# The row of maxima sent from ScalarE's queue, and a new order of instructions up to tile 2

## The chip, the core and the metric

The kernel runs on one core of a Trainium2 chip. The metric is the device time of one execution in microseconds (us), without the host. A core has TensorE (PE; matrix products, in the profile also PEld, the weight loads), VectorE (DVE), ScalarE (ACT), GpSimd (POOL) and SyncE (SP), which here only issues DMAs. An engine works through its instructions in program order; engines wait for each other through semaphores. DMAs can be issued by SP, ACT and POOL, each on its own queue, and all of them run on the core's 16 DMA engines. Matmul results go to PSUM, eight banks; other tiles lie in SBUF.

## What is computed

Attention with a decay bias over 8 batches, 8 heads, 576 positions and 64 dimensions, then Fourier mixing over positions and channels, a layer norm and an MLP of 512 to 2048 to 512, all in float32:

```python
scores = scale * np.matmul(q, k.transpose(0, 1, 3, 2))
cum = np.cumsum(np.maximum(s, 0.0), axis=-1)
bias = -(cum[:, :, :, None] - cum[:, :, None, :])
scores = np.where(causal, -1000000000.0, scores + np.minimum(bias, 0.0))
scores = scores - np.max(scores, axis=-1, keepdims=True)
attn = np.exp(scores)
attn = attn / (np.sum(attn, axis=-1, keepdims=True) + 1e-09)
x = np.matmul(attn, v)            # heads side by side: 8 x 576 x 512
mixed = np.real(np.fft.fft(np.fft.fft(x, axis=1), axis=2))
u = x + mixed
un = (u - mu) / np.sqrt(var + 1e-06)
out = u + np.maximum(un @ w_ch1, 0.0) @ w_ch2
```

## The kernel before

The 64 heads are worked through as 32 pairs. Of each pair the kernel loads q and k transposed (`qk`, line 947) and rounds them to the high part that TensorE's one-pass float32 takes (`KQ`, `high()`, lines 964 and 966); the rest goes to `q` and `k` (`low()`, lines 981 to 989, partly by DMA), the values to `va` (line 992). `KQ` has 128 partitions: 64 carry the head's dimensions, of the others three carry the bias (`cumD`, line 961) and the maximum, so that one matmul gives q times k plus bias minus maximum.

The maximum has to be known ahead of the scores. `maxes(i)` multiplies q and k once with 128 queries on the partitions (`pm`, line 1005), takes the largest of each row on VectorE (`Mx`, `M`, lines 1007 and 1009), turns the nine columns of maxima into rows on TensorE (`pmt`, line 1038), copies them out of PSUM on ScalarE (`mt`, 9 x 128, line 1040) and writes them by DMA into partition 2 of `KQ` (line 1041). This happens for pairs 1 to 31, 31 sends of 4.5 KB; pair 0 goes another way (line 1031). `scores(i)` computes keys by queries (`ps`, lines 1061, 1062 and 1071), ScalarE takes the exponential (`P`, lines 1063 and 1073), GpSimd cuts the causal corner (line 920). `av(i)` multiplies by the values (`pavA`, `pavB`, lines 1094 and 1097), ScalarE copies the result (`stage`, `sumrow`, lines 1099 to 1102), and SP sends the sums on (line 1105); `recip` and `finish` divide (`rd`, `rb`, `xa`, `xs`, `xr`, lines 1111 to 1139). The pairs overlap: beside the scores of pair i run the maxima of pair i + 1, the rounding of pair i + 2, the values of pair i - 1 and the division of pair i - 2.

In the same stage the weights of the MLP are rounded (`raw`, `we`, `wm`, `wD`, lines 505 to 525), GpSimd loads the tables of the Fourier step (lines 733 to 737), and every fourth pair ends a batch, which is folded and mixed (`folds`, `fourier`, lines 753 to 849). Then come the layer norm (`ln_tile`, lines 579 to 626) and the MLP in nine tiles of 512 tokens (`mlp_tile`; `h` line 660, `zh` and `zl` lines 664 and 665, `acc` lines 673 to 675, `out` line 708). Tiles 0 and 1 are done in two halves of the weights each, tile 2 is the fifth part.

The order of instructions up to the end of tile 2 isn't the order of the code. `order()` takes all instructions traced so far, gives each a duration (`cost()`), plays the five engines through, picks for each engine the next instruction and chains each engine's list, so that the program keeps it. Of those that can start within `SLACK[engine]` ns of the earliest, it takes the one of lowest rank: its place in the code, shifted by `SHIFT[engine, tile]` (seven numbers, one for each phase: the first three pairs, the four turns of pairs to a batch, the last pair, and what follows) and by a draw from `SEED`. `SLOTS` says which buffer or PSUM bank each tile takes. Data dependencies and buffers hold in any order; the tables decide only what goes first. For a DMA the play counts 650 ns on the engine that issues it, 1945 ns until it moves, its transfer on a `link`, and 284 ns until it has landed. Before the change all queues share one `link`. From tile 3 on the instructions follow the code.

The three lines that end `maxes()`:

```python
mt = att.tile([9, 128], F32R, tag="mt", name="mt", bufs=2)
nc.scalar.copy(mt, p[0:9, 0:128])
nc.sync.dma_start(out=flat(qy)[2:3].bitcast(F32).rearrange("o (c t) -> o c t", t=128), in_=mt.bitcast(F32))
```

Of the kernel before, what the change touches and what calls it, by code (L numbers as in the profile page):

```python
# [59 lines left out]
SLACK = {PE: 14.0, ACT: 41.0, POOL: 155.0, SP: 10.0}  # L60
SHIFT = {
    (PE, "acc"): (0, 0, 0, 0, 0, 0, 48), (PE, "h"): (0, 0, 0, 0, 0, 0, -9), (PE, "mu"): (0, 12, 0, 0, 0, 0, 18), (PE, "p"): (0, 0, 0, 0, 2059, 0, 6),
    (PE, "pavA"): (0, 1, -4, 48, 0, 0, 0), (PE, "pavB"): (0, -1, -6, 0, 0, -51, 0), (PE, "pm"): (-1333, -6145, 0, -32, 0, 0, 0),
    (PE, "pmt"): (3, -2, 0, -18, -56, 0, 0), (PE, "ps"): (3, 0, 0, 0, 0, 0, 0), (PE, "pyc"): (0, 0, 0, 0, 0, 5, 5),
    (PE, "pys"): (0, 0, 0, 0, 0, -737, -5), (PE, "pzc"): (0, 0, -4179, 16, 0, -5, 112), (PE, "pzs"): (0, 0, 0, 0, 0, 466, 18),
    (PE, "var"): (0, 0, 0, 0, 0, 541, 70),
    (DVE, "Aw"): (116, 0, 0, 0, 366, -15, 0), (DVE, "De"): (0, 0, 0, 0, 0, -16, 0), (DVE, "Df"): (0, 0, 0, 0, 139, -685, 0),
    (DVE, "Dg"): (0, -773, 0, 0, -190, -12, 0), (DVE, "Do"): (0, -210, 0, 0, 0, 227, 0), (DVE, "Ds"): (0, 6, 0, 0, 729, 17, 0),
    (DVE, "KQ"): (231, 0, 0, 0, 0, 0, 0), (DVE, "M"): (-276, 0, -281, 307, 70, 0, 0), (DVE, "Mx"): (0, -3905, 922, -46, 0, 0, 0),
    (DVE, "cumhl"): (-135, 0, 0, 0, 0, 0, 0), (DVE, "cw"): (352, 0, 0, 0, 0, 0, 0), (DVE, "e"): (0, 0, 0, 0, 446, -421, 0),  # L70
    (DVE, "el"): (0, 0, 0, 0, 0, 492, 0), (DVE, "eps"): (-535, 0, 0, 0, 0, 0, 0), (DVE, "k"): (198, 52, 430, 177, 135, 0, 0),
    (DVE, "m"): (0, 0, 0, 0, 0, 0, 403), (DVE, "ones"): (267, 0, 0, 0, 0, 0, 0), (DVE, "r"): (0, 0, 0, 0, 0, 6609, 0),
    (DVE, "rows"): (0, 0, 0, 0, 487, 0, -94), (DVE, "s"): (0, 0, 0, 0, 0, 0, 5), (DVE, "skip"): (-4, 0, 0, 0, 0, 0, 0),
    (DVE, "sums"): (0, 0, 697, 301, -764, -14, 0), (DVE, "t"): (0, -1413, 0, 0, 0, -122, 2531), (DVE, "tl"): (0, 0, 0, 0, 0, -473, 385),
    (DVE, "trash"): (0, 0, 238, -17, -3399, 0, 0), (DVE, "tt"): (0, 0, 0, 0, 0, 0, 772), (DVE, "u"): (0, -132, 0, 0, 0, 0, 1031),
    (DVE, "ucl"): (0, 3907, 0, 0, 0, 0, 866), (DVE, "wbias"): (263, 0, 0, 0, 0, 0, 0), (DVE, "we"): (22, 37, 88, -98, 29, 0, -193),
    (DVE, "wl"): (0, 0, 0, 0, 0, -12, -374), (DVE, "wm"): (29, -94, 1640, 3733, -32, 0, 1395), (DVE, "xr"): (0, 0, 0, 0, 0, 241, 0),
    (DVE, "ym"): (0, 0, 0, 0, 1034, -117, 1601), (DVE, "yp"): (0, 0, 0, 0, -1302, 0, -140), (DVE, "z"): (0, 0, -37, -850, 0, -61, 69),
    (DVE, "zc"): (0, 0, -295, 30, 0, -124, -270), (DVE, "zl"): (0, 0, 0, 0, 0, 0, 136), (DVE, "zs"): (0, 0, 10, 0, 0, -2535, -181),
    (ACT, "De"): (0, 0, 0, 0, -178, -334, 0), (ACT, "Do"): (0, -181, 0, 0, 0, 21, 0), (ACT, "KQ"): (464, 2119, -62, 56, 0, 0, 0),  # L80
    (ACT, "P"): (1000, 5, 22, -43, 1058, 0, 0), (ACT, "Px"): (-244, -2956, 222, -126, -23, 0, 0), (ACT, "e"): (0, 0, 0, 0, 2330, 69, 0),
    (ACT, "el"): (0, 0, 0, 0, -91, -325, 0), (ACT, "k"): (-171, 0, 0, 0, 0, 0, 0), (ACT, "m"): (0, 0, 0, 0, 0, 0, 353),
# [1 line left out]
    (ACT, "q"): (-336, 0, 0, 0, 0, 0, 0), (ACT, "r"): (0, 0, 0, 0, 0, 309, -145), (ACT, "stage"): (284, 0, 5478, -80, -1805, -180, 0),
    (ACT, "sumrow"): (2, -5148, -306, -9, -13, -511, 0), (ACT, "th"): (0, -86, 0, 0, 0, -306, 553), (ACT, "u"): (0, 909, 0, 0, 0, 0, 683),
    (ACT, "uch"): (0, 157, 0, 0, 0, 0, -1053), (ACT, "we"): (368, 0, -932, 603, 27, 0, 0), (ACT, "wh"): (0, 0, 0, 0, 0, 55, 580),
    (ACT, "yc"): (0, 0, 0, 9, -179, -417, 120), (ACT, "zc"): (0, 0, 4, 50, 0, -548, 0), (ACT, "zh"): (0, 0, 0, 0, 0, 0, 106),
    (ACT, "zs"): (0, 0, 0, 0, 0, 0, 84),
    (POOL, "Bw"): (0, -1371, 0, 0, 6, 0, 0), (POOL, "Dg"): (0, -333, 0, 0, 656, 0, 0), (POOL, "KQ"): (-829, 0, 0, 0, 0, 0, 0),
    (POOL, "P"): (129, 53, 307, 4346, -632, 0, 0), (POOL, "Px"): (-18, 655, 614, 132, -728, 0, 0), (POOL, "cor"): (0, 0, 0, 0, 114, 0, 0),  # L90
    (POOL, "dtab"): (0, -80, 0, 468, 0, 0, 0), (POOL, "ident"): (318, 0, 0, 0, 0, 0, 0), (POOL, "o"): (0, 0, 0, 0, 0, 0, 64),
    (POOL, "q"): (-2496, 9, 2193, 652, 163, 0, 0), (POOL, "stab"): (0, 0, 135, 0, -254, 0, 0), (POOL, "t"): (0, 243, 0, 0, 0, 0, 42),
    (POOL, "tri"): (87, 0, 0, 0, 0, 0, 0), (POOL, "trih"): (-332, 0, 0, 0, 0, 0, 0), (POOL, "w"): (0, 0, 0, 0, 0, 0, 387),
    (POOL, "we"): (487, -87, -612, 717, -286, 0, -131), (POOL, "wl"): (0, 0, 0, 0, 0, -748, 0), (POOL, "xa"): (0, 0, 0, 0, 76, 0, 273),
    (POOL, "xr"): (0, 0, 0, -216, 0, 131, 0), (POOL, "xs"): (0, 112, 0, 0, 747, 511, 0),
    (SP, "KQ"): (-1596, 1213, -3572, -104, 203, 0, 0), (SP, "aD"): (0, 0, 0, 0, 0, 0, -353), (SP, "c"): (0, 0, 0, 0, 0, 0, -1400),
    (SP, "cumD"): (-24, 0, 0, 0, 0, 0, 0), (SP, "cw"): (470, 0, 0, 0, 0, 0, 0), (SP, "eh"): (0, 0, 0, 0, -343, 0, 0),
    (SP, "k"): (0, 598, 3460, -298, 72, 0, 0), (SP, "md"): (0, 0, 0, 0, 0, 0, -1671), (SP, "mu"): (0, 0, 0, 0, 0, 0, -411),
    (SP, "out_0_dram"): (0, 0, 0, 0, 0, 0, 319), (SP, "part"): (0, 0, 0, 0, 0, 0, -28), (SP, "q"): (-37, 409, 2316, -468, -91, 0, 0),
    (SP, "qk"): (571, -8, -258, -596, 407, 0, 0), (SP, "r"): (0, 0, 0, 0, 0, 0, -583), (SP, "raw"): (51, 280, 605, 0, 4131, 0, -292),  # L100
    (SP, "rb"): (0, -55, -491, 4, 389, 0, 0), (SP, "rd"): (0, 238, -4561, -38, 275, 50, 0), (SP, "rows"): (0, -51, 0, 0, 0, 22, 0),
    (SP, "sd"): (0, 0, 0, 0, 0, 0, -366), (SP, "sums"): (-235, 279, -3399, 749, -782, 0, 0), (SP, "uD"): (0, 0, 0, 0, -56, -243, 0),
    (SP, "uch"): (0, 0, 0, 0, 0, 0, 292), (SP, "va"): (244, 2263, -100, 0, -98, 0, 0), (SP, "wD"): (127, 2697, -2392, 497, 187, 0, 0),
    (SP, "wl"): (0, 0, 0, 0, 0, 930, -73), (SP, "xa"): (0, 0, 86, 0, 0, 186, 0), (SP, "xs"): (0, -306, 0, -1581, 0, 0, 0),
}
SEED = (0, 31, 29586, 2585, 51369, 44703, 14542, 16155, 37996, 368, 58769, 58696, 10048, 26897, 8812, 6379, 13084, 28209, 37780, 34222, 0, 1533,
    35176, 40344, 52354, 710, 54698, 781, 37426, 44411, 28381, 1858, 0, 0, 0)
SLOTS = {
    "P": (
        "0213210321032103210321032103210321302130213021302130213021302130213"  # L110
# [5 lines left out]
        "012340123403124031403412034210321042104203140410420432043210202104314321402301301423014213043043021302143012324312032032"  # L116
        "413014201341034123043124031240031240321032020320321432413201320413023410234034201342302301301340321421421021302132043204"
        "321421342310043104104310423101204104130234102402142421342130201320430412301402402310231402312142012012340123413241212012"
        "410343104302430243103201432132401324040321423140123420142042042024132321341341304321031030430143024102103230230320041431"
        "414124120413042304343043104201342013"  # L120
    ),
    "bank": (
        "012012012012012012012012012012012012012012012012012012012012010210210210210210210210120120101010212101201020210101201212"
        "012122012020202022020210202101012010102101012121201212012121021010101010102102121212012012012010120202102121021212012020"
        "202020202020101001201202021020210102102121021212102121202020202020202102021201021012120210210212012020012010101010101010"
        "121202102102102120202212012010101212121202021021021021021020012012010120121201201201201201201201201201201201201201202102"
        "10"
    ),
# [1277 lines left out]
```

## Time and profile before

| | us |
|---|---|
| timed runs | 1307.12, 1311.54, 1311.57 |
| their median | 1311.54 |
| the profiled execution | 1306.26 |
| its span, first to last instruction | 1304.5 |
| mean granted TensorE clock in it | 0.987 |

The profile is of one execution, whose own time lies below the timed runs. Its pages name an instruction by its line and by the tile it writes and reads (`KQ<-mt`). `PEclk` is the share of full speed that TensorE's throttle granted; DMA share is the mean busy share of the 16 DMA engines. Times within the trace count from the start of the span. An engine's wait is put down to what released it.

### The profile page before, as it was taken

Reading aid. Unit: us, or ns where it says so; the run is one execution under the profiler, and the core shown is the slowest. Engines: PE = TensorE matmul, PEld = TensorE weight load, DVE = VectorE, ACT = ScalarE, POOL = GpSimd, SP = SyncE. Lnnn points to the kernel's source line nnn. Section 1 sums busy time; section 2 is a strip of 40 time slices with the busy share of each in tenths; the row PEclk is TensorE's granted clock in tenths of the full one; section 3 lists DMA queues with packets and bytes.
Section 4 is the critical chain, followed back from the end, with each engine's and each line's share of the span. In section 5 each row is a group of like instructions: output and inputs, shape, how many; then the busy total and the mean of one; then the engine's idle time right before and its main releaser. Section 6 shows DMA issues by size and latency. Waiting matters only on the chain.

```text
span 1304.5 us, 17902 instructions
## 1 busy us (share of the span) xinstructions
PE 1247.2 (96%) x6205; PEld 1004.3 (77%) x6205; DVE 730.5 (56%) x1720; ACT 514.4 (39%) x1115; POOL 568.7 (44%) x529
## 2 busy tenths in 40 slices
PE   5998999999999989989999999999999999999998
PEld 4765777777787767878777888888888888888886
DVE  7889997989878878677744222322323323223212
ACT  5776785777677654434320211211212112112110
POOL 7566766777866864334645022130141221301510
PEclk9999999999999989999999999999999999999999
DMA  6877767576556453454333003022040130220300
GB/s 181 226 214 173 208 175 185 158 211 186 162 155 171 136 160 117 131 92 139 101 62 122 9 17 114 9 85 62 1 137 9 25 114 9 77 71 1 105 1 33
DMA packets 118469, 141.70 MB, mean 109 GB/s; under 512 B 51103, under 2 KB 75319, under 8 KB 116587
## 3 DMA queue, kind: packets, MB, share of 16 engines
q1 hardware_dynamic: 116887, 137.14, 38.1%
q0 software_dynamic: 672, 1.98, 0.6%
q10 hardware_dynamic: 820, 1.45, 0.4%
q8 instruction: 49, 0.80, 0.3%
q14 instruction: 41, 0.34, 0.1%
HBM read 77.13 MB, written 25.31 MB: 79 GB/s over the span
## 4 chain that ended last, share of the span: by engine, by line
PE 78%; DMA 7%; DVE 6%; POOL 3%; ACT 2%; issue 2%; SPq 1%; DVEq 0%; POOLq 0%; ACTq 0%
PE h L660 27%; PE acc L675 9%; PE acc L673 9%; PE acc L674 9%; PE pavB L1094 7%; PE ps L1061 3%; PE pm L1005 3%; PE ps L1062 3%; PE pavA L1094 2%; PE pyc L826 1%; DMA raw<-in_wP_dram 1%; DMA sd<-s 1%; DMA sums<-stage 1%; PE pys L835 1%; DMA KQ<-mt 1%
## 5 line engine op out<-in xcount | busy, mean ns | idle before, releaser
L665 DVE SCALAR_TENSOR_TENSOR zl<-h,zh 128x512 fp32r<-128x512 f32 x144 | 99.2, 690 | 367.6 <-ACT zh L664 367.4
L664 ACT ACTIVATE zh<-h 128x512 fp32r<-128x512 f32 x144 | 85.7, 597 | 487.1 <-PE h L660 395.1
L675 PE MATMUL acc<-zl,wh 128*128 128x512 f32 x577 | 226.4, 393 | 5.6 <-DVE zl L665 5.6
L673 PE MATMUL acc<-zh,wh 128*128 128x512 f32 x577 | 226.4, 393 | 1.9 <-ACT zh L664 1.9
L674 PE MATMUL acc<-zh,wl 128*128 128x512 f32 x577 | 225.7, 391 | 0.0
L660 PE MATMUL h<-uch,wh 128*128 128x512 f32 x576 | 161.4, 392 | 3.2 <-DVE zl L665 2.4
L660 PE MATMUL h<-ucl,wh 128*128 128x512 f32 x576 | 162.7, 392 | 0.0
L660 PE MATMUL h<-uch,wl 128*128 128x512 f32 x576 | 160.1, 393 | 0.0
L1094 PE MATMUL pavB<-P,va 128*65 128x320 f32 (+1 forms) x512 | 156.0, 408 | 0.9 <-ACT stage L1102 0.4
L1063 ACT ACTIVATE P<-ps 128x320 f32<-128x320 f32 (+3 forms) x320 | 126.0, 425 | 56.7 <-PE ps L1062 52.1
L707 POOL TENSOR_TENSOR o<-o,w 128x512 f32<-128x512 f32 x32 | 43.0, 1344 | 211.0 <-issue 209.1
L1005 PE MATMUL pm<-KQ 128*128 128x320 f32 (+4 forms) x352 | 114.9, 388 | 19.0 <-ACT KQ L966 12.6
L675 PEld LDWEIGHTS acc<-zl,wh 128*128 128x128 f32 x577 | 109.0, 189 | 30.5 <-DVE zl L665 7.5
L1061 PE MATMUL ps<-KQ 128*128 128x256 f32 (+4 forms) x352 | 121.2, 356 | 8.0 <-ACT P L1063 4.3
L660 PEld LDWEIGHTS h<-uch,wh 128*128 128x128 f32 x576 | 107.4, 188 | 27.6 <-DVE zl L665 2.8
L673 PEld LDWEIGHTS acc<-zh,wh 128*128 128x128 f32 x577 | 109.3, 189 | 25.0 <-ACT zh L664 2.3
L674 PEld LDWEIGHTS acc<-zh,wl 128*128 128x128 f32 x577 | 109.4, 190 | 23.2
L660 PEld LDWEIGHTS h<-ucl,wh 128*128 128x128 f32 x576 | 109.2, 190 | 23.4
L660 PEld LDWEIGHTS h<-uch,wl 128*128 128x128 f32 x576 | 108.8, 189 | 23.4
L1009 DVE CUSTOM_DVE_ANT_0 trash<-pm,tri 128x320 bf16<-128x320 f32 (+2 forms) x256 | 117.1, 482 | 10.6 <-PE pm L1005 8.8
L989 POOL TENSOR_TENSOR q<-qk,q 64x576 fp32r<-64x576 f32 x64 | 96.7, 1526 | 27.3 <-DMA q<-KQ 16.1
L1062 PE MATMUL ps<-q,k 128*128 128x256 f32 (+4 forms) x352 | 105.8, 311 | 0.0
(179 smaller groups left out, 2014.2 us busy)
## 6 DMA issues: line engine op xcount, KB each, us to landing
qk<-in_qkT_dram SPq DMA_DIRECT2D x32, 576.0 KB
raw<-in_wP_dram SPq DMA_DIRECT2D x64, 256.0 KB
va<-in_vA_dram SPq DMA_DIRECT2D x32, 325.0 KB
rb<-rd SPq DMA_DIRECT2D x64, 144.0 KB
k<-KQ SPq DMA_DIRECT2D x31, 288.0 KB
q<-KQ SPq DMA_DIRECT2D x31, 288.0 KB
u<-uD SPq DMA_DIRECT2D x8, 1024.0 KB
out_dram<-o SPq DMA_DIRECT2D x32, 256.0 KB
```

Of the source, the lines that this page charges most:

```text
L660: nc.tensor.matmul(h[:, :n], a[:, j * 128:(j + 1) * 128], b[:, j, :n], start=i == 0, stop=i == 11)
L665: nc.vector.scalar_tensor_tensor(out=zl[:, :n], in0=h[:, :n], scalar=0.0, in1=zh[:, :n].bitcast(F32), op0=ALU.max, op1=ALU.subtract)
L673: nc.tensor.matmul(acc[j][:, u:v], a[:, cs], y[:, u:v], start=g == lo, stop=False)
L674: nc.tensor.matmul(acc[j][:, u:v], b[:, cs], y[:, u:v], start=False, stop=False)
L675: nc.tensor.matmul(acc[j][:, u:v], a[:, cs], z[:, u:v], start=False, stop=g == hi - 1 and v == n)
L989: nc.gpsimd.tensor_sub(q1[64:128, h], qk[0:64, h], q1[0:64, h].bitcast(F32))
L1005: nc.tensor.matmul(p[:, :n], q, keys, start=True, stop=True)
L1009: nc.vector.tensor_tensor_reduce(out=next(turn)[:, :n], in0=p[:, :n], in1=mask, scale=1.0, scalar=NEG, op0=ALU.add, op1=ALU.max, accum_out ...
L1061: nc.tensor.matmul(p[:, u:v], flat(ky)[:, k0:k0 + 128], flat(qy)[:, m:m + v - u], start=True, stop=False)
L1062: nc.tensor.matmul(p[:, u:v], flat(k1)[:, k0:k0 + 128], flat(q1)[:, m:m + v - u], start=False, stop=True)
L1063: nc.scalar.activation(P[:, POFF[c] + a:POFF[c] + a + n], p[:, :n], AF.Exp, scale=0.125)
L1094: nc.tensor.matmul(p[:65, u - lo:n], va[:, c, 65 * h:65 * h + 65], P[:, o:o + lo + n - u], start=c == 0, stop=c == 1 and tg == "A")
```

## The change

Line 1041 issues the row from ScalarE. In `order()` the transfers of each queue count on a `link` of their own. The tables `SLACK`, `SHIFT`, `SEED` and `SLOTS` are replaced as a whole (the diff shows a few of their lines); `SLOTS` keeps `qk` and `stage` and changes the sequence of buffers for `P`, `m` and `bank`. No other instruction is added, removed or changed.

```diff
-SLACK = {PE: 14.0, ACT: 41.0, POOL: 155.0, SP: 10.0}
+SLACK = {PE: 21.0, ACT: 119.0, POOL: 208.0, SP: 67.0}
...
-    (ACT, "mt"): (-138, 1388, -1253, 76, 78, 0, 0), (ACT, "mu"): (0, 0, 0, 0, 0, 0, -21), (ACT, "part"): (0, 0, 0, 0, 0, 0, 3389),
+    (ACT, "mt"): (0, -214, -414, 14, -2403, 0, 0), (ACT, "mu"): (0, -29, 0, 0, 0, 0, -36), (ACT, "q"): (48, 0, 0, 0, 0, 0, 0),
...
-    "P": (
-        "0213210321032103210321032103210321302130213021302130213021302130213"
+    "P": (
+        "0213210321032103210321032103210321032103210321032103210321032103210"
...
-    link, landed, taken, result = 0.0, [], set(), {e: [] for e in ENGINES}
+    link, landed, taken, result = dict.fromkeys(ENGINES, 0.0), [], set(), {e: [] for e in ENGINES}
...
-            link = max(begin + 1945, link) + s.link
-            end = link + 284
+            link[e] = max(begin + 1945, link[e]) + s.link
+            end = link[e] + 284
...
-        nc.sync.dma_start(out=flat(qy)[2:3].bitcast(F32).rearrange("o (c t) -> o c t", t=128), in_=mt.bitcast(F32))
+        nc.scalar.dma_start(out=flat(qy)[2:3].bitcast(F32).rearrange("o (c t) -> o c t", t=128), in_=mt.bitcast(F32))
```

More of the change, by code (lines that the diff above doesn't have):

```diff
@@ L59 @@
 }
-SLACK = {PE: 14.0, ACT: 41.0, POOL: 155.0, SP: 10.0}
+SLACK = {PE: 21.0, ACT: 119.0, POOL: 208.0, SP: 67.0}
 SHIFT = {
[L62 to L82, printed above, removed]
-    (ACT, "mt"): (-138, 1388, -1253, 76, 78, 0, 0), (ACT, "mu"): (0, 0, 0, 0, 0, 0, -21), (ACT, "part"): (0, 0, 0, 0, 0, 0, 3389),
[L84 to L104, printed above, removed]
-}
@@ L106 @@
-SEED = (0, 31, 29586, 2585, 51369, 44703, 14542, 16155, 37996, 368, 58769, 58696, 10048, 26897, 8812, 6379, 13084, 28209, 37780, 34222, 0, 1533,
-    35176, 40344, 52354, 710, 54698, 781, 37426, 44411, 28381, 1858, 0, 0, 0)
+    (PE, "acc"): (0, 0, 0, 0, 0, 0, 48), (PE, "h"): (0, 0, 0, 0, 0, 0, -9), (PE, "mu"): (0, -549, 0, 0, 0, 0, 33),
+    (PE, "p"): (0, 0, 0, 0, -3, 0, -19), (PE, "pavA"): (0, -6, 0, 50, 0, 0, 0), (PE, "pavB"): (0, 0, -6, 0, 0, -745, 0),
+    (PE, "pm"): (-1248, -5998, -5, -33, 0, 0, 0), (PE, "pmt"): (-364, -959, -1922, -282, -234, 0, 0), (PE, "pyc"): (0, 0, 0, -2, -8, 1296, 1),
@@ new lines @@
+    (PE, "pys"): (0, 0, 0, 0, 0, 14, -6), (PE, "pzc"): (0, 0, -6246, -103, 0, 88, 8), (PE, "pzs"): (0, 0, -2786, 0, 0, 150, 0),
+    (PE, "var"): (0, 0, 0, 0, 0, 1887, 141),
+    (DVE, "Aw"): (523, 0, 0, 0, -321, 75, 0), (DVE, "De"): (0, 0, 0, 0, -177, -4073, 0), (DVE, "Df"): (0, 0, 0, 0, -1030, -2559, 0),
+    (DVE, "Dg"): (0, 0, 0, 0, 0, -5130, 0), (DVE, "Do"): (0, -79, 0, 0, 0, -90, 0), (DVE, "Ds"): (0, 0, 0, 0, 182, -218, 0),
+    (DVE, "KQ"): (212, 0, 0, 0, 0, 0, 0), (DVE, "M"): (-1689, -2, 10, 401, -3837, 0, 0), (DVE, "Mx"): (-57, -26, 122, -4, -1672, 0, 0),
@@ new lines @@
+    (DVE, "cumhl"): (-264, 0, 0, 0, 0, 0, 0), (DVE, "cw"): (-624, 0, 0, 0, 0, 0, 0), (DVE, "e"): (0, 0, 0, 0, 808, -990, 0),
+    (DVE, "eh"): (-286, 0, 0, 0, 0, 0, 0), (DVE, "el"): (0, 0, 0, 0, -40, -203, 0), (DVE, "eps"): (67, 0, 0, 0, 0, 0, 0),
+    (DVE, "k"): (0, 753, 718, -2, 45, 0, 0), (DVE, "o"): (0, 0, 0, 0, 0, 0, 47), (DVE, "ones"): (-206, 0, 0, 0, 0, 0, 0),
+    (DVE, "part"): (0, 0, 0, 0, 0, 0, -88), (DVE, "r"): (0, 0, 0, 0, 0, 107, -1322), (DVE, "rows"): (0, 0, 0, 0, -184, 0, 17),
@@ new lines @@
+    (DVE, "s"): (0, 0, 0, 0, 0, 0, -54), (DVE, "skip"): (145, 0, 0, 0, 0, 0, 0), (DVE, "sums"): (0, 530, 603, 0, -1807, -96, 0),
+    (DVE, "t"): (0, -44, 0, 0, 0, -44, 7123), (DVE, "tl"): (0, 37, 0, 0, 0, 0, 0), (DVE, "trash"): (-1248, -9, 0, -7, -6039, 0, 0),
+    (DVE, "tt"): (0, 0, 0, 0, 0, 0, -158), (DVE, "u"): (0, 435, 0, 0, 0, 0, 692), (DVE, "ucl"): (0, -202, 0, 0, 0, 0, -3226),
+    (DVE, "wbias"): (-16, 0, 0, 0, 0, 0, 0), (DVE, "we"): (-1338, -20, -60, 129, -139, 0, -1825), (DVE, "wl"): (0, 0, 0, 0, 0, -62, -1027),
@@ new lines @@
+    (DVE, "wm"): (-232, -84, 1794, -110, 40, 0, 1111), (DVE, "xr"): (0, 0, 0, 0, 0, 470, 0), (DVE, "ym"): (0, 0, 0, 0, 987, 385, 105),
+    (DVE, "yp"): (0, 0, 0, 0, 0, -161, -111), (DVE, "z"): (0, 0, -879, -279, 0, 239, 48), (DVE, "zc"): (0, 0, -600, 120, 0, 0, 0),
+    (DVE, "zl"): (0, 0, 0, 0, 0, 0, 55), (DVE, "zs"): (0, 0, -732, 0, 0, -1, 317),
+    (ACT, "De"): (0, 0, 0, 0, -76, -1909, 0), (ACT, "Do"): (0, 36, 0, 0, 0, 110, 0), (ACT, "KQ"): (1117, 406, -38, 1201, 847, 0, 0),
+    (ACT, "P"): (0, -9, -3559, 0, 1826, 0, 0), (ACT, "Px"): (-36, 1028, -304, -2895, -159, 0, 0), (ACT, "e"): (0, 0, 0, 0, 3604, -597, 0),
@@ new lines @@
+    (ACT, "el"): (0, 0, 0, 0, 0, -1339, 0), (ACT, "k"): (2792, 0, 0, 0, 0, 0, 0), (ACT, "m"): (0, 0, 0, 0, 0, 0, 27),
+    (ACT, "mt"): (0, -214, -414, 14, -2403, 0, 0), (ACT, "mu"): (0, -29, 0, 0, 0, 0, -36), (ACT, "q"): (48, 0, 0, 0, 0, 0, 0),
+    (ACT, "r"): (0, 0, 0, 0, 0, -195, 1), (ACT, "stage"): (887, 0, 5637, 0, 0, 0, 0), (ACT, "sumrow"): (0, -6650, 716, 137, 13, 221, 0),
+    (ACT, "th"): (0, 0, 0, 0, 0, -22, -142), (ACT, "u"): (0, 393, 0, 0, 0, 0, 0), (ACT, "uch"): (0, 0, 0, 0, 0, 0, -32),
@@ new lines @@
+    (ACT, "we"): (0, -121, 5, 556, 0, 0, -249), (ACT, "wh"): (0, 0, 0, 0, 0, -322, -50), (ACT, "yc"): (0, 0, 0, 54, 0, 55, 368),
+    (ACT, "zc"): (0, 0, -3207, 1171, 0, 842, -541), (ACT, "zh"): (0, 0, 0, 0, 0, 0, -442), (ACT, "zs"): (0, 0, 0, 0, 0, 373, -858),
+    (POOL, "Bw"): (0, 0, 0, 0, 371, 170, 0), (POOL, "Dg"): (0, -158, 0, 0, 413, 382, 0), (POOL, "KQ"): (-197, 0, 0, 0, 0, 0, 0),
+    (POOL, "P"): (228, -135, -405, -25, -163, 0, 0), (POOL, "Px"): (806, 1810, -172, -3043, -1514, 0, 0), (POOL, "dtab"): (0, 439, 0, 153, 0, 0, 0),
@@ new lines @@
+    (POOL, "ident"): (83, 0, 0, 0, 0, 0, 0), (POOL, "o"): (0, 0, 0, 0, 0, 0, -104), (POOL, "q"): (-2308, 0, 2623, 0, 486, 0, 0),
+    (POOL, "stab"): (0, 0, 39, 0, 13, 0, 0), (POOL, "t"): (0, 425, 0, 0, 0, 711, -3646), (POOL, "tri"): (-606, 0, 0, 0, 0, 0, 0),
+    (POOL, "trih"): (238, 0, 0, 0, 0, 0, 0), (POOL, "we"): (0, -25, 1938, -843, -625, 0, 50), (POOL, "wl"): (0, 0, 0, 0, 0, 22, -516),
+    (POOL, "xa"): (0, 0, 0, 0, -1259, 0, 211), (POOL, "xr"): (0, 0, 0, -85, 0, -546, 0), (POOL, "xs"): (0, -2579, 0, 0, 2176, 1125, -65),
@@ new lines @@
+    (SP, "KQ"): (-172, 4484, 486, 0, -200, 0, 0), (SP, "aD"): (0, 0, 0, 0, 0, 0, 24), (SP, "c"): (0, 0, 0, 0, 0, 0, -316),
+    (SP, "cumD"): (-316, 0, 0, 0, 0, 0, 0), (SP, "eh"): (0, 0, 0, 0, 782, -25, 0), (SP, "k"): (196, 64, 3069, 1455, 35, 0, 0),
+    (SP, "md"): (0, 0, 0, 0, 0, 0, -476), (SP, "out_0_dram"): (0, 0, 0, 0, 0, 0, 16), (SP, "part"): (0, 0, 0, 0, 0, 0, -324),
+    (SP, "q"): (-474, 26, 2008, 1016, -157, 0, 0), (SP, "qk"): (14, 0, 58, -132, 1758, 0, 0), (SP, "r"): (0, 0, 0, 0, 0, 0, -259),
@@ new lines @@
+    (SP, "raw"): (253, -2, -12, -109, 4312, 0, 0), (SP, "rb"): (0, -276, 0, 0, 1356, 33, 0), (SP, "rd"): (0, 0, 129, -3865, 0, -445, 0),
+    (SP, "rows"): (0, -97, 0, 0, 0, -91, 0), (SP, "sums"): (-171, 1853, -2736, 834, -2286, -46, 0), (SP, "u"): (0, 0, 0, 0, 0, 0, -65),
+    (SP, "uD"): (0, 0, 0, 0, -327, -152, 0), (SP, "uch"): (0, 0, 0, 0, 0, 0, -445), (SP, "va"): (84, 0, -194, 161, 0, 0, 0),
+    (SP, "wD"): (-153, 425, -22, 1101, 108, 0, 0), (SP, "wl"): (0, 0, 0, 0, 0, 0, 450), (SP, "xa"): (0, 0, 0, 0, 0, 553, 0),
@@ L108 @@
+    (SP, "xs"): (0, 12, 0, 0, 0, 0, 0),
+}
+SEED = (0, 0, 50255, 35777, 31526, 18710, 59161, 610, 10617, 4271, 57241, 9164, 15699, 35378, 48528, 43316, 33796, 50044, 23544, 47454, 31404, 14786,
+    45807, 45356, 56577, 59650, 39205, 44802, 35412, 54142, 3304, 19498, 48914, 0, 0)
 SLOTS = {
     "P": (
-        "0213210321032103210321032103210321302130213021302130213021302130213"
+        "0213210321032103210321032103210321032103210321032103210321032103210"
     ),
@@ L115 @@
     "m": (
[L116 to L120, printed above, removed]
+        "012340123403142031203241031240324012401204130301313241324013023402140214021232321212124140203030210214021034120341231204"
+        "310212012423140423103030421032410341231243234234230121204130413041231042310214023104231042302143021423042314310423012102"
+        "143243120431420143213214320124124302430214304043032013201243131340320432034313134323401234012431240134013024104210201230"
+        "124312341241240124301423010431204132121024304310421320321020142014231312323232032041014301203120143240240141342013243043"
+        "013013010324034030312043120420314203"
     ),
     "bank": (
[L123 to L127, printed above, removed]
+        "012012012012012012012012012012012012012012012012012012012012010210210210210210210210202102121220120121201021021221021010"
+        "210101021010012012012012020221021021021220201010210202022222102120120120120120101020201201201020200102102121021212120101"
+        "201201212012020201201202012101021210210202021212102121212012012012012012120210210201012020202010120101101020201201201201"
+        "202012012120120102020101010212121010101202020202101010212010210210212102102102102102102102102102102102102102102102101201"
+        "20"
     ),
```

## The prediction

> **What bounds the kernel now.** I read the table of busy times first, then the busy time by stage, then the chain that ended last, and last the waits of TensorE's weight loads.
>
> ```profile
> span 1304.5 us, 17902 instructions
> PE 1247.2 (96%) x6205; PEld 1004.3 (77%) x6205; DVE 730.5 (56%) x1720; ACT 514.4 (39%) x1115; POOL 568.7 (44%) x529
> PE 78%; DMA 7%; DVE 6%; POOL 3%; ACT 2%; issue 2%; SPq 1%; DVEq 0%; POOLq 0%; ACTq 0%
> ```
> ```profile
> core 0: us, PE busy (x) PEld busy (x) DVE busy (x) ACT busy (x) POOL busy (x), PEclk, DMA share, GB/s
> 0.00:26.00 26.00, 12.08 (x54) 9.49 (x54) 22.53 (x63) 13.03 (x20) 22.01 (x28) 1.00 0.59 172
> 26.00:450.00 424.00, 404.11 (x2472) 314.16 (x2471) 364.76 (x1044) 305.81 (x719) 291.33 (x283) 0.99 0.68 183
> 450.00:500.00 50.00, 40.04 (x191) 30.25 (x191) 40.46 (x72) 29.49 (x65) 33.15 (x29) 0.89 0.52 170
> 500.00:750.00 250.00, 242.29 (x1073) 196.67 (x1073) 154.19 (x309) 79.12 (x166) 101.08 (x101) 0.98 0.34 91
> 750.00:1304.50 554.50, 548.67 (x2421) 453.71 (x2419) 148.61 (x233) 86.95 (x146) 121.11 (x90) 1.00 0.18 51
> ```
>
> TensorE is busy for 96% of the span and holds 78% of the chain. The rows by stage say where the other 57 us are: 13.9 before the first scores, 19.9 in the attention stage (26 to 450 us), 10.0 between attention and MLP, 7.7 in the first MLP tiles, 5.8 behind that. The change works on the plan up to tile 2, so on what lies before about 750 us. The matmuls stay as they are; only idle time and half-clock time can be won or lost. Half clock is small: 1 less the granted clock, times busy time, gives about 4 us at 26 to 450 us (0.01 x 404), 4.4 at 450 to 500 (0.11 x 40) and 4.8 at 500 to 750 (0.02 x 242).
>
> ```profile
> PEld ps L1061 <- ACT P L1063: 8.5, 14, 1.8
> PEld pm L1005 <- DVE Mx L1009: 7.4, 14, 1.3
> PEld ps L1061 <- DMA KQ<-mt: 4.4, 4, 2.2
> L1041 SPq DMA_DIRECT2D KQ<-mt x31: 798/825/1662, 26.5 to 442.8; - x31
> PE h L660 27%; PE acc L675 9%; PE acc L673 9%; PE acc L674 9%; PE pavB L1094 7%; PE ps L1061 3%; PE pm L1005 3%; PE ps L1062 3%; PE pavA L1094 2%; PE pyc L826 1%; DMA raw<-in_wP_dram 1%; DMA sd<-s 1%; DMA sums<-stage 1%; PE pys L835 1%; DMA KQ<-mt 1%
> 202.70 8.13 DMA KQ<-mt
> 237.92 3.38 DMA KQ<-mt
> 389.44 1.94 DMA KQ<-mt
> ```
>
> The first three rows (total, times, longest) are waits of the weight loads, the last three pieces of the chain (start, length), below its shares by line. The row of maxima is sent 31 times and made TensorE wait in only 4, 4.4 us in all. Three pieces of it lie on the chain. The shortest, 1.94 us, shows an undisturbed send; the longest took 6.2 us more. What lay before that one stands in the timeline of the DMA queue:
>
> ```profile
> 200.78 0.36 SPq L947 DMA_DIRECT2D qk<-in_qkT_dram  x1
> 201.19 0.43 SPq L505 DMA_DIRECT2D raw<-in_wP_dram  x1
> 201.71 0.52 SPq L981 DMA_DIRECT2D q<-KQ  x1
> 202.70 0.83 SPq L1041 DMA_DIRECT2D KQ<-mt  x1
> 202.70:210.80 8.10, 5.85 (x32) 3.92 (x30) 8.02 (x29) 3.49 (x7) 3.79 (x6) 1.00 1.05 235
> 210.00:220.00 10.00, 9.12 (x53) 8.42 (x54) 3.33 (x9) 5.54 (x15) 6.30 (x7) 0.83 0.58 156
> ```
> ```profile
> qk<-in_qkT_dram SPq DMA_DIRECT2D x32, 576.0 KB
> raw<-in_wP_dram SPq DMA_DIRECT2D x64, 256.0 KB
> q<-KQ SPq DMA_DIRECT2D x31, 288.0 KB
> u<-uD ACTq DMA_DIRECT2D x1, 1024.0 KB
> ```
>
> In the 2 us before it SP had issued 576 + 256 + 288 = 1120 KB; at the 235 GB/s of those 8.1 us that is 4.9 us of transfers ahead of 4.5 KB. The delay is a queue of transfers, not the send. The idle TensorE then ran part of the next 10 us at half clock (0.83 granted of 9.12 us busy: 1.6 us).
>
> **Does ScalarE's queue pass that backlog?** Everything hangs on it, and the trace has one place that shows it, since the load of u (1024 KB) already goes out from ScalarE:
>
> ```profile
> 442.69 0.40 ACTq L579 DMA_DIRECT2D u<-uD  x1
> 442.81 0.83 SPq L1041 DMA_DIRECT2D KQ<-mt  x1
> 442.70:443.70 1.00, 1.00 (x5) 0.51 (x4) 1.00 (x3) 0.41 (x2) 0.64 (x1) 1.00 0.07 23
> 443.70:447.50 3.80, 3.80 (x22) 2.17 (x20) 3.69 (x6) 3.01 (x8) 3.80 (x4) 1.00 0.96 261
> 448.48 0.30 PE L1061 MATMUL ps<-KQ 128*128 128x64 f32 x1
> ```
>
> ScalarE issued u 0.12 us before SP issued a row of maxima. In 443.7 to 447.5 us the engines moved 261 x 3.80 = 992 KB (of 1000 bytes), about u's 1049 of the same; little is left for anything else. The matmul that reads the row started at 448.48, 5.7 us after the issue against 1.94 for the undisturbed send. So the small transfer of one queue very likely stood behind the large one of the other: the two hardware queues seem to be served in order of issue. I take it that ScalarE's queue gives the row no way past SP's backlog. It is one place, and the other way round (SP large, ScalarE small) is not in the trace.
>
> The Trainium skill has a rule for each answer. Its page "DMA: Bandwidth & Descriptors", section "Queues, rings and completion order", says that each DMA engine takes turns between the queue rows that have work, packet by packet; by that rule a 4.5 KB row on another queue passes at once, the first rival below. The same page, section "Issuing engines are not separate DMA queues", says that issuing from several engines saves only the sequencer's issue time; that speaks against a gain here. The windows above agree with the second and not with the first.
>
> **The change part by part**, against the profiled execution (1306.26 us with a span of 1304.5; what lies around the span, 1.8 us, doesn't change).
>
> 1. SP loses 31 issues x 0.825 us = 25.6 us, and the waits for `mt` that stood at the head of its in-order queue. What is behind them (rb, va, k, cumD in the code's terms) goes out earlier. TensorE hardly waits for these: among its longest waits the row of maxima is the only DMA. Bounds: 0, and the 13 us that the chain gives to the sums that SP sends (1% of the span in the page's list by line). I take -1, near the end that TensorE's waits show.
> 2. The row itself. It leaves right behind the copy instead of behind SP's other work, but meets the same backlog. Bounds: the whole wait and its half clock gone, -4.4 - 1.6 = -6.0; on the other side, rows planned as if nothing lay ahead and late, +6.2 for each as late as the one at 202.70. I take -1.5: a third of the wait, as SP's turn goes and the backlog stays.
> 3. ScalarE gains 31 issues, and each stands between a copy of `mt` and the next exponential, which gives PSUM banks back to the scores. ScalarE's own issues in the trace are of other shapes:
>
> ```profile
> L959 ACTq DMA_DIRECT2D KQ<-cumhl x1: 1184/1184/1184, 8.7 to 8.7; - x1
> 9.96 1.24 ACT L979 CAST k<-qk 64x576 fp32r<-64x576 f32 x2 [2.84 <-issue]
> 150.00:200.00 50.00, 48.91 (x317) 39.77 (x316) 46.62 (x142) 38.23 (x92) 37.49 (x38) 1.00 0.71 198
> 350.00:400.00 50.00, 49.57 (x318) 39.63 (x317) 42.42 (x124) 35.84 (x86) 34.85 (x32) 1.00 0.64 170
> 400.00:450.00 50.00, 49.55 (x315) 38.65 (x312) 40.95 (x112) 33.25 (x82) 36.23 (x36) 1.00 0.54 148
> 200.00:250.00 50.00, 45.00 (x260) 34.09 (x259) 41.11 (x108) 32.34 (x77) 33.17 (x33) 0.97 0.62 162
> ```
>
>    One issue takes 0.40 (u) to 1.18 us (KQ), and the second row shows that ScalarE computes nothing meanwhile. I use SP's 0.83 for the same send: 25.6 us over 417 us, 3.1 in each 50. In 150 to 200 us ScalarE has 50 - 38.2 = 11.8 us free, so its own idle time can hold it; queued behind are P, stage and KQ copies, for which the scores and the maxima wait. If free time falls by 3.1/11.8 = 26%, the 8.5 us of waits for P grow by about 2.2. Bounds: 0 (all in idle time) and +25.6 (all on the path). I take +2, by the waits that exist.
> 4. The plan counts transfers per queue (`link[e]`), so SP's transfers beside u, and those beside the tables that GpSimd loads, come later than it expects. Bounds: 0, and +3.8, the window that u filled. I take +1, since one such load meets waiting work on all engines.
> 5. The order anew. Same instructions, same durations, other places. The bounds are stages of this trace: at the pace of 350 to 450 us TensorE idles 0.88 us in 100, so 3.7 in 424 instead of 19.9: -16. At that of 200 to 250 it idles 5.0 in 50, so 42 in 424: +22. I take -4, a quarter of the better bound: the best stages show that an order without holes exists, but they are those with the lightest DMA load (148 and 170 GB/s against 183), and where the plan's transfers differ from the chip's, new holes open.
>
> Sum: -1 - 1.5 + 2 + 1 - 4 = **-3.5**, so 1302.8 for an execution like the profiled one. The three timed runs are 1307.12, 1311.54 and 1311.57; the profiled execution lies below all. Their mean with it is 1309.1, 2.9 above it. I add these: 1302.8 + 2.9 = **1305.7 us**, 0.45% under the median before.
>
> **Rivals.**
>
> - *The queues pass each other.* The row lands as fast as at 389.44 everywhere, and the plan can put scores earlier. For it: 31 sends with up to 6.2 us of delay. Against: the window of u. Worth -6.0 for the row, -1 for SP, +2 for ScalarE, -8 for the order (half of the better bound, since the plan's transfers would then be the chip's): -13, so 1306.26 - 13 + 2.9 = **1296 us**.
> - *The row is late where the plan thinks it early* (slower). Place: the first score matmul of a pair of heads. The plan lets nothing but ScalarE's own sends delay the row; served in order of issue it stands behind SP's, and TensorE, in order, stands with it. One like 202.70 costs 6.2 us and 1.6 us of half clock, 7.8. One more than now, with parts 1, 3, 4 and 5 as above (-2) and no gain on the row: +5.8, 1314.9, still within 0.5%. Two: +13.6, **1323 us**. It decides from the second such row. For it: 1120 KB in 2 us is not a rare load at 183 GB/s. Against: today just 4 rows of 31 were waited for.
> - *The row changes hands, nothing else.* It goes from ScalarE, lands as before, and the order is as good as the old one (part 5 is nothing): -1 - 1.5 + 2 + 1 = +0.5, **1309.7 us**. For it: 4.4 us of waits is all that hung on the row. Against: 30 us of idle time before 500 us leave room.
>
> **How the numbers follow.** A measurement of this kernel tells about 0.5% from no change, 6.6 us: faster is below 1304.98, slower above 1318.1. Forecast 0.45 (0.17 faster, 0.27 same, 0.01 slower; its own range 1301 to 1311); queues that pass 0.25 (0.22 faster, 0.03 same); nothing else 0.17 (0.01, 0.14, 0.02); late rows 0.13 (0.01 same, 0.12 slower). Together 0.40 faster, 0.45 same, 0.15 slower. The range goes from 1295, which leaves out the better part of the first rival (0.1), to 1320, which takes in one late row and a part of the way to two, and leaves out about 0.09.
>
> **What would show it.** Right: TensorE's idle time at 26 to 450 us down from 19.9 to about 16, waits on `KQ<-mt` of 2 to 4 us, sends of 0.8 us on ScalarE's queue, waits for P near 10 us, and a row issued right behind SP's big loads that still takes over 4 us. Wrong: such a row arriving within 2 us (queues pass), waits on `KQ<-mt` above 10 us (late rows), or waits for P above 15 us, which would put ScalarE's issues on the path. A change behind 750 us would be against all of this.

## The result and the profile after

| | before | after |
|---|---|---|
| timed runs, median (us) | 1311.55 | 1324.98 |
| lowest to highest | 1307.12 to 1314.67 | 1323.16 to 1329.01 |
| ratio | | 1.0109, 95% interval 1.0071 to 1.0147 |
| profiled execution (us) | 1306.26 | 1326.03 |

The change made the kernel about 1.1% slower. A second measurement, beside fresh runs of before (median 1303.33), gave 1318.44 and a ratio of 1.0120 (1.0091 to 1.0149). Both kernels ran faster in that session, so it is the ratios that compare, not the times. The forecast was 1305.7 in a range of 1295 to 1320.

The head of the page after, and its table of busy times by stage (columns as before):

```profile
span 1324.3 us, 17916 instructions
PE 1255.1 (95%) x6205; PEld 1005.0 (76%) x6205; DVE 731.5 (55%) x1720; ACT 518.0 (39%) x1115; POOL 566.6 (43%) x529
```
```profile
26.00:450.00 424.00, 396.56 (x2383) 303.48 (x2384) 349.35 (x1016) 299.86 (x694) 279.94 (x271) 0.98 0.67 177
450.00:500.00 50.00, 44.70 (x248) 34.42 (x246) 42.68 (x80) 31.83 (x76) 33.39 (x32) 0.93 0.46 148
500.00:750.00 250.00, 234.55 (x1020) 189.40 (x1021) 164.78 (x326) 85.04 (x176) 110.95 (x110) 0.97 0.35 104
750.00:1324.30 574.30, 567.95 (x2503) 468.97 (x2501) 152.76 (x237) 87.88 (x149) 119.88 (x90) 1.00 0.17 50
```

The span is 19.8 us longer in these two executions. TensorE did the same 6205 matmuls, but was idle for 1324.3 - 1255.1 = 69.2 us (before 57.3) and busy for 7.9 us more, with the mean granted clock at 0.983 (before 0.987). The attention stage is behind: by 450 us 2383 of its matmuls had run against 2472. The waits of TensorE's weight loads (total, times, longest), and the sends themselves (shortest, median, longest in ns):

```profile
PEld ps L1060 <- DMA KQ<-mt: 15.4, 10, 6.3
PEld pm L1004 <- POOL KQ L908: 11.7, 1, 11.7
PEld ps L1060 <- ACT P L1062: 8.3, 16, 2.1
PEld pm L1004 <- DVE Mx L1008: 7.0, 12, 1.9
```
```profile
L1040 ACTq DMA_DIRECT2D KQ<-mt x31: 722/723/793, 25.1 to 457.3; - x31
```

Waits on the row of maxima went from 4.4 us in 4 to 15.4 in 10, 11.0 us more, nearly all the added idle time (11.9). The second measurement's profile has 14.9 us in 12. Waits on P, where ScalarE's sends would show, are what they were (8.3 against 8.5). The 11.7 us is the wait for the first matmul of the kernel, which was there before under another name (12.5 us).

The longest wait shows how it happens. The timeline after (start, length; an x2 is two issues merged), with DMA issues of three queues and the matmul that waited:

```profile
62.37 1.24 SPq L504 DMA_DIRECT2D raw<-in_wP_dram  x2
63.85 0.59 POOL L732 DMA_DIRECT2D stab<-in_tabS_dram  x1
64.56 0.79 SPq L960 DMA_DIRECT2D KQ<-cumD  x1
65.46 0.34 SPq L946 DMA_DIRECT2D qk<-in_qkT_dram  x1
65.91 0.60 SPq L980 DMA_DIRECT2D q<-KQ  x1
66.34 0.74 ACTq L1040 DMA_DIRECT2D KQ<-mt  x1
...
76.04 0.42 PE L1060 MATMUL ps<-KQ 128*128 128x64 f32 x1 [5.89 <-DMA KQ<-mt]
```

ScalarE sent the row 0.03 us after its copy of `mt` ended (66.05 + 0.26): nothing was in its way on its own queue. In the 4 us ahead of it SP had issued 2 x 256 + 27 + 576 + 288 KB and GpSimd a table of 659 KB. TensorE stood for 5.9 us at a row of 4.5 KB, which came 9.7 us after its issue. Then it ran at part of its clock: a 128x256 score matmul took 0.41 us at 77.06, 0.28 us at 62.80. The stages around it, after:

```profile
50.00:100.00 50.00, 41.84 (x234) 31.30 (x233) 36.20 (x112) 33.61 (x78) 25.45 (x28) 0.93 0.76 179
100.00:150.00 50.00, 44.83 (x245) 32.08 (x245) 40.35 (x114) 31.70 (x76) 31.05 (x30) 0.90 0.67 175
```

Before, both had the full clock (1.00). Here 0.07 x 41.8 + 0.10 x 44.8 = 7.4 us went to the lower clock. Over the whole span the same sum is 0.013 x 1247 = 16 us before and 0.017 x 1255 = 21 us after, so some 5 us more; elsewhere the changed kernel lost less. In the second measurement's profile the stage from 100 to 150 us had its full clock. So this profile reads as waits on late rows and a lower clock behind them. The experiments ask how much of the loss that is.

### The profile page after: what moved, and what is told of

Read it like the earlier page. It is cut to its first block, busy times and chain, and to the rows that moved or that the text cites. A ratio compares the mean times of both kernels' runs of the same rounds, so it can differ in the third digit from the quotient of the medians.

```text
span 1324.3 us, 17916 instructions
## 1 busy us (share of the span) xinstructions
PE 1255.1 (95%) x6205; PEld 1005.0 (76%) x6205; DVE 731.5 (55%) x1720; ACT 518.0 (39%) x1115; POOL 566.6 (43%) x529
## 4 chain that ended last, share of the span: by engine, by line
PE 52%; DMA 6%; issue 5%; DVE 4%; POOL 1%; ACT 1%; SPq 0%; ACTq 0%; DVEq 0%; POOLq 0%
PE h L659 23%; PE acc L674 8%; PE acc L672 8%; PE acc L673 8%; DMA raw<-in_wP_dram 2%; PE pavB L1093 1%; DMA sd<-s 1%; PE ps L1060 1%; DMA out_dram<-o 1%; PE ps L1061 1%; DVE zl L664 1%; DMA KQ<-mt 1%; PE pavA L1093 1%; PE pyc L825 0%; PE pm L1004 0%
## 5 line engine op out<-in xcount | busy, mean ns | idle before, releaser
L1060 PE MATMUL ps<-KQ 128*128 128x256 f32 (+4 forms) x352 | 120.2, 352 | 17.0 <-DMA KQ<-mt 11.7
```

The lines of the kernel that those rows point to most:

```text
L1060: nc.tensor.matmul(p[:, u:v], flat(ky)[:, k0:k0 + 128], flat(qy)[:, m:m + v - u], start=True, stop=False)
```

## The experiments

Three theories. **Late rows:** the row stands behind other queues' transfers, and the plan, which counts it on an empty link, puts the score matmuls where it isn't there yet. **ScalarE:** its 31 issues hold up P. **Order:** the new lists are worse by themselves. The plan can be told to put the row where it would stand on one engine and have another issue it, so that all other lists stay, instruction by instruction. Ratios are against before, with their 95% interval.

**Only the hand.** Before's order; the row, planned on SP, is put into ScalarE's list at the same moment:

```diff
-    users = depend(steps)
+    row = [s for s in steps if s.kind == "InstDMACopy" and label(s.reads[0].tensor) == "mt"]; [setattr(s, "engine", SP) for s in row]; users = depend(steps)
...
-        result[e].append(s)
+        result[ACT if s in row else e].append(s)
...
-        nc.sync.dma_start(out=flat(qy)[2:3]...
+        nc.scalar.dma_start(out=flat(qy)[2:3]...
```

> The order of before on every engine, instruction by instruction; only the 31 sends of the row of maxima are issued by ScalarE, each at the place in time that the plan gave SP. Late rows (the row stands behind SP's transfers on either queue, and the new plan doesn't know it): this plan does know it, so within 4 us of before, 1307 to 1315, waits of TensorE on KQ<-mt near 4 us. ScalarE's issues on the path: 10 us or more above before, waits for P well above 8.5 us. The order is to blame alone: as before.

1.0030 (1.0005 to 1.0055). The waits, of TensorE's weight loads:

```profile
PEld ps L1061 <- ACT P L1063: 9.4, 19, 2.1
...
PEld ps L1061 <- DMA KQ<-mt: 0.2, 1, 0.2
```

The wait for the row is gone, 0.2 us for 4.4, where the first theory had it near 4, and the time isn't better but a little worse. The same kernel again:

> e1_hand once more, since its interval (1.0005 to 1.0055) left open whether ScalarE's issues cost anything: with 31 issues of 0.73 us partly on the path 1.002 to 1.005; wholly hidden 0.998 to 1.001, which would put e1_hand's 0.3% down to its session.

1.0026 (1.0005 to 1.0047): 0.3%, some 3.5 us. So ending nearly all waits for the row gained nothing here. The hand alone, in the old order, costs about a quarter of the 1.2%.

**Only the order.** After's lists, the row back on SP (the same edit the other way round, planned on ScalarE):

> The order of after on every engine; only the 31 sends are issued by SP again, each at the place in time that the plan gave ScalarE. Late rows: as slow as after, 1320 or more, with waits on KQ<-mt of 10 us or more, since the rows are still planned as if nothing lay ahead. ScalarE's issues on the path: back to 1312 or less. The order is to blame alone: as slow as after, but with waits on KQ<-mt near 4 us.

1.0266 (1.0221 to 1.0311).

```profile
PEld ps L1060 <- DMA KQ<-mt: 30.1, 13, 9.6
```

The new order is bad without ScalarE's sends too, and worse: waits on the row double. In this order ScalarE's queue helps; the loss isn't its issues. That SP would make the waits so much longer I had not expected.

**Only the play.** The changed kernel with the one link of before:

```diff
-            link[e] = max(begin + 1945, link[e]) + s.link
-            end = link[e] + 284
+            link = max(begin + 1945, link) + s.link
+            end = link + 284
```

> The changed kernel with its tables and its queue, but the plan counts all transfers on one link again, so it expects the row behind SP's backlog. The order changes with it. Late rows: waits on KQ<-mt fall from 15 us to 6 or less, and the time by at least 6 us, to 1319 or less. ScalarE's issues on the path, or tables that are bad by themselves: 1322 to 1328 as after.

and the kernel before with a link for each queue:

> The kernel before with its tables, the row on SP, and only the plan's links taken apart, one for each queue. Late rows: the row is on SP's own link and still counted behind SP's transfers, so waits on KQ<-mt stay near 4 us; only what runs beside the load of u and the tables of the Fourier step is misjudged, 0 to 5 us above before, 1309 to 1316. Links apart spoil the order whatever the row does: 1320 or more.

1.0379 (1.0327 to 1.0431) and 1.0338 (1.0295 to 1.0380). The waits on the row in the one and the other:

```profile
PEld ps L1060 <- DMA KQ<-mt: 5.3, 4, 3.7
```
```profile
PEld ps L1061 <- DMA KQ<-mt: 4.0, 4, 1.4
```

The waits came out as the first theory has it: with the row counted behind SP's transfers, 5.3 us for 15.4. The times didn't: both are far slower, by other waits. I had taken the tables for something that survives an edit of the play; they don't. So neither run separates the theories by its time. The change's code with before's tables shows the size of that:

> The change's two edits in the code (the row on ScalarE's queue, a link for each queue), with SLACK, SHIFT, SEED and SLOTS of the kernel before. The tables fit only the play for which they were made: 1335 or more, as e4_links (1350) and e3_one_link (1354), so the new tables win back a part of what the new play costs. The tables carry over: 1305 to 1328, no worse than the changed kernel.

1.0503 (1.0478 to 1.0528). Its longest waits:

```profile
PEld pavA L1094 <- POOL P L920: 18.6, 1, 18.6
...
PEld pm L1005 <- DVE Mx L1009: 14.4, 14, 6.7
```

The new play with old tables loses 5%; with the new tables three quarters of that are won back, and the kernel stops 1.2% above before.

**Without waiting for rows.** From pair 3 on the row goes where nobody reads; the plan is told what stood there, so all lists stay (after's below; before's in the same way, with `nc.sync`). These kernels leave out the maximum and so don't compute the reference's result; they tell of time alone:

```diff
-        nc.scalar.dma_start(out=flat(qy)[2:3]..., in_=mt.bitcast(F32))
+        row = flat(qy)[2:3]...; nc.scalar.dma_start(out=row if i < NR else dram.tile([9, 128], F32, tag="spare", name="spare", bufs=2), in_=mt.bitcast(F32)); PLANNED[list(nc.all_instructions())[-1].name] = [mt], [row]
...
-        nc.sync.dma_start(out=cumD[2, 1], in_=zero)
+        nc.sync.dma_start(out=cumD[2, 1], in_=cumhl[:R, 0:S].bitcast(F32)); PLANNED[list(nc.all_instructions())[-1].name] = [zero], [cumD[2, 1]]
...
+        self.reads, self.writes = PLANNED.get(ins.name, (self.reads, self.writes))
```

> The order of after on every engine and all its instructions, but from pair 3 on the row of maxima is sent to a tile in DRAM that nobody reads; partition 2 of KQ holds the running sum of the decay from the start instead, which the softmax cancels, so no score matmul waits for a row. Late rows are the loss: 15.4 us of waits and about 7 us of half clock go with them, 1303 to 1312. The order is worse by itself, rows or not: 1318 or more.

> The same edit in the kernel before, its order kept: the rows go where nobody reads, and no score matmul waits for one. Its rows cost 4.4 us of waits and 1.6 us of half clock: 3 to 7 us under before. If it stands more than 5 us under the changed kernel with the same edit, the order of after is worse apart from its rows; if the two agree, the rows are the whole difference.

After's order: 1.0045 (1.0026 to 1.0065). Before's: 1.0005 (0.9987 to 1.0023), where I had expected 3 to 7 us less. Two readings. The rows cost the kernel before nothing that can be measured (at most some 2 us), so there was next to nothing to win by sending them faster. And with them gone, after's order still stands 0.4% above before's. The stages around the longest wait, in after's order without it:

```profile
50.00:100.00 50.00, 47.80 (x279) 35.32 (x278) 41.30 (x129) 39.49 (x91) 30.67 (x32) 1.00 0.83 207
100.00:150.00 50.00, 45.34 (x265) 33.69 (x263) 42.46 (x127) 35.15 (x83) 32.00 (x31) 0.93 0.68 187
```

At 50 to 100 us the clock is full again and TensorE busy for 47.8 us, as before the change (47.7). But a send to DRAM took ScalarE 0.27 us, not 0.72, so this run took away some of ScalarE's load as well. Two runs settle that: the unread rows on SP, so that ScalarE sends nothing, and unread rows that take ScalarE as long as the real ones (to a second partition of `sumrow`):

> f1_after_no_row with its 31 unread rows issued by SP at the same places, so ScalarE has no sends; partition 2 of KQ is filled as there. ScalarE's issues cost the 0.3% that e1_hand showed: 1.001 to 1.002 of before, against 1.0045 for f1_after_no_row. The order's other places cost it: 1.0045 as before.

> f1_after_no_row with its 31 sends as long for ScalarE as those of the changed kernel: the unread rows go to a second partition of sumrow, in the same nine pieces of 512 bytes, not to DRAM (there an issue took 0.27 us in place of 0.73). Partition 2 of KQ is filled as there. Waiting for late rows is the loss: 1.004 to 1.007 of before, as f1_after_no_row. ScalarE's issues carry a part of it: 1.008 to 1.012.

1.0056 (1.0037 to 1.0075) without sends on ScalarE and 1.0058 (1.0032 to 1.0083) with 29 of full length:

```profile
L1040 ACTq DMA_DIRECT2D sumrow<-mt x29: 722/725/752, 51.7 to 451.2; - x29
```

The three agree, so in this order ScalarE's issues cost nothing that can be seen, within some 4 us. With the same sends, waited for or not, the kernel stands at 1.0120 (1.0091 to 1.0149; the second measurement, whose expectation follows) or 1.0058: waiting for rows costs 0.6%, about 8 us of the 15.6 (3 to 13 with both intervals). These two intervals don't meet; that of the first measurement (from 1.0071) touches the 1.0083. The other 0.5%, 1.0058 less the 1.0005 of before's order, is about 7 us (3 to 11): the new order's other places.

The stage from 50 to 100 us doesn't recover in every run without waits for rows. In the last two (first ScalarE without sends, then with full ones) TensorE idles there all the same:

```profile
50.00:100.00 50.00, 42.95 (x227) 30.73 (x225) 37.79 (x108) 33.54 (x78) 28.05 (x31) 0.90 0.76 187
50.00:100.00 50.00, 43.33 (x239) 30.62 (x237) 37.94 (x115) 34.59 (x79) 28.78 (x32) 0.97 0.77 198
```

The longest wait there is in both for the maxima themselves (4.1 and 4.0 us): TensorE is to turn them (`pmt`) before VectorE has them (`Mx`). Over the whole run, in before's order without rows and in after's with unread rows of full length:

```profile
PEld pmt L1038 <- DVE Mx L1035: 1.5, 3, 1.0
PEld pmt L1037 <- DVE Mx L1034: 7.8, 8, 4.0
```

The four profiles of the old order have 1.5 to 2.4 us of this wait, the six of the new one (the row on either queue, waited for or not) 4.4 to 9.7. So one of the other places is named by the traces. That it makes the 7 us isn't shown: a wait seen isn't time won, as the row's own waits in the old order show.

> The changed kernel as it is, beside the next three, so that all stand against the same runs of before: 1.0 to 1.4% over it. With it the rows' part (this less f1_after_no_row) has one footing.

**The queues by themselves.** A small kernel loads tiles of 576 KB from one queue and then sends a row of 4.5 KB from another. The first try waited in the wrong place and its loads were too small, so it decides nothing:

> Not the kernel: it loads one or two tiles of 576 KB from one queue, then sends a row of 4.5 KB from another, and VectorE waits for the row; each case twice, output left at constants. Queues served in order of issue: behind two large loads of SP the row arrives as late from ScalarE's queue as from SP's, some 4 us or more later than alone (1152 KB at 235 GB/s are 5 us, less the 1.5 us by which the loads are ahead), and the same the other way round. Queues that pass each other: from ScalarE's queue within 1 us of the row sent alone.

> As m1_queues, with up to six loads of 576 KB ahead of the row and ScalarE itself waiting for it, since two loads were nearly done when the row went out and VectorE waited for the loads first. Queues served in order of issue: behind six loads of SP the row comes at least 4 us later than alone, from ScalarE's queue as from SP's, and the same with six loads on ScalarE's queue and the row on SP's. Queues that pass each other: within 1 us of the row sent alone when row and loads are on different queues, and late only when both are on one.

Timeline of the second, in its second repetition: the row's issue, and ScalarE's copy of it, with the time that it waited for it. Alone from ScalarE and from SP; behind six loads of SP from ScalarE and from SP; behind six loads of ScalarE from SP and from ScalarE:

```profile
156.81 0.74 ACTq L49 DMA_DIRECT2D rowax<-mt  x1
158.70 1.15 ACT L50 COPY seen<-rowax 1x1152 f32<-1x1152 f32 x1 [1.92 <-DMA rowax<-mt]
163.59 0.73 SPq L49 DMA_DIRECT2D rowbx<-mt  x1
165.47 1.15 ACT L50 COPY seen<-rowbx 1x1152 f32<-1x1152 f32 x1 [1.90 <-DMA rowbx<-mt]
...
186.23 0.74 ACTq L49 DMA_DIRECT2D rowex<-mt  x1
191.96 1.15 ACT L50 COPY seen<-rowex 1x1152 f32<-1x1152 f32 x1 [5.76 <-DMA rowex<-mt]
206.93 0.75 SPq L49 DMA_DIRECT2D rowgx<-mt  x1
214.92 1.15 ACT L50 COPY seen<-rowgx 1x1152 f32<-1x1152 f32 x1 [8.02 <-DMA rowgx<-mt]
235.34 0.75 SPq L49 DMA_DIRECT2D rowix<-mt  x1
240.00 1.15 ACT L50 COPY seen<-rowix 1x1152 f32<-1x1152 f32 x1 [4.68 <-DMA rowix<-mt]
247.99 0.73 ACTq L49 DMA_DIRECT2D rowjx<-mt  x1
252.62 1.15 ACT L50 COPY seen<-rowjx 1x1152 f32<-1x1152 f32 x1 [4.66 <-DMA rowjx<-mt]
```

From issue to copy it is 1.9 us alone on either queue. Behind SP's six loads it is 5.7 us from ScalarE's queue and 8.0 from SP's own. So ScalarE's queue passes a part of SP's loads: it saves 2.3 of 6.1 us, and the row is still 3.8 us late. The first repetition shows which part. GpSimd copies from each of the six loads as it lands; the row sent from ScalarE at 58.31 was copied at 64.03, between the fourth load and the fifth:

```profile
58.04 0.18 POOL L52 COPY past<-big 128x1 f32<-128x1 f32 x1 [4.10 <-DMA big<-in_qkT_dram]
58.31 0.73 ACTq L49 DMA_DIRECT2D rowex<-mt  x1
...
63.41 0.18 POOL L52 COPY past<-big 128x1 f32<-128x1 f32 x1 [1.20 <-DMA big<-in_qkT_dram]
64.03 1.15 ACT L50 COPY seen<-rowex 1x1152 f32<-1x1152 f32 x1 [5.75 <-DMA rowex<-mt]
64.85 0.18 POOL L52 COPY past<-big 128x1 f32<-128x1 f32 x1 [1.26 <-DMA big<-in_qkT_dram]
66.24 0.18 POOL L52 COPY past<-big 128x1 f32<-128x1 f32 x1 [1.20 <-DMA big<-in_qkT_dram]
```

The other way round, with the loads further ahead, both rows are late alike in this repetition (4.7 us from SP, 4.6 from ScalarE; in the first 4.9 and 5.7), and SP's row came when the sixth load did, within 0.3 us: that fits an order of issue. Behind six loads of GpSimd's queue a row from SP or ScalarE took 5.0 to 5.3 us in three tests (6.7 in the fourth, while SP stored the output); a table of GpSimd stood ahead of the row at 66.34 too, and no run tells its part of that delay from SP's. "In order of issue" was too strong for SP's loads ahead of ScalarE's row; "each queue for itself", as the new plan has it, fits none of these tests.

## Why the prediction was wrong, step by step

The time came out above the range, and on the side that the prediction gave 0.15. The second rival was the mechanism: the row late where the plan thinks it early. Its place (the first score matmul of a pair) was right, and its time, 1323, was 2 us from the measured 1324.98. That closeness is luck. It counted two rows at 6.2 us of wait and 1.6 us of lower clock; measured were ten waits of 1.5 us on average, the longest 6.3 (in the second profile twelve, the longest 3.5). And it came to its time by rows alone; the runs give the rows about 8 us and the rest of the order about 7.

- **The row itself, taken at -1.5, failed.** It cost about +8. The gain wasn't there to begin with: without any wait for rows before's order stands at 1.0005, so the bound of -6.0, waits and lower clock summed from the trace, was no bound of time. The step held that the row "meets the same backlog" and still took a third of the wait as won. The same text had the plan counting the row on an empty link, so the plan would no longer leave room for that backlog. What was weighed against late rows, "today just 4 rows of 31 were waited for", came from a plan that counted it, and couldn't speak for one that doesn't.
- **The order anew, taken at -4, failed.** It cost about +7, inside its bounds of -16 to +22. The value was set by the best stages of the old trace. With the old tables the new play gives 1.0503, so the new tables had some 65 us to win back before they could gain; nothing in the profile of before showed that, and I didn't ask what the tables are worth outside the play they were fitted to.
- **ScalarE, +2**: nothing seen in the new order, some +3.5 in the old one (with SP's relief in it). In the new order the runs resolve some 4 us, so +2 is neither shown nor refuted there.
- **SP's relief, -1**: not seen by itself. In the old order it and ScalarE's issues together are +0.3%.
- **The links apart, +1**: its reason, a load of u that holds up SP, was seen in the small kernel too, but the price was taken for one place. No run has it by itself. What it did to the whole order is in the two steps above.
- **The reading of the queues** was right in what it needed: ScalarE's queue gives no free way past SP's backlog. It gives some, 2.3 of 6.1 us. The Trainium skill's page "DMA: Bandwidth & Descriptors", section "Queues, rings and completion order", has the engines take turns between queues; its section "Issuing engines are not separate DMA queues" has nothing saved but issue time. The small kernel agrees with neither in full (8.0 us on SP's own queue, 5.7 from ScalarE's, 1.9 alone).
- **What would show it**: waits on `KQ<-mt` above 10 us were named as the sign of late rows, and the profile has 15.4. Waits for P stayed at 8.3. A sign named for being right came as well, a row behind SP's loads that took over 4 us (9.7); it tells of the queues, not of the time.

What stays open: which of the new order's other places cost the 7 us. The traces point at TensorE's wait for `Mx`, but single profiles of one kernel differ by several us (1326.03 and 1314.20 for the changed one), and no run took those places apart. It is also open why the hand alone costs 0.3% in the old order; both its profiles have some 2 us of waits for `KQ<-cumD`, which SP sends. None of the kernels here is faster than the one before.

## What to carry to other kernels

When a plan is made by playing a model through, an edit of the model is an edit of the whole order: ask first what the new model leaves out that the old one had, since that is where the plan will be early. Waits left in the trace are what the plan didn't foresee; that they are few says nothing of a plan that stops foreseeing them. And before moving a transfer to win a wait, take the wait away altogether: here, in the old order, that gained nothing (1.0005), which was the ceiling.
